# Modulating the first token tile behind its transposes, by columns, in a fused adaLN block

## The chip, the cores and the metric

The kernel runs on one core of a Trainium2 chip. A core has TensorE (PE, the matrix engine, with its weight loads listed apart as PEld), VectorE (DVE), ScalarE (ACT), GpSimd (POOL) and SyncE (SP, which here issues most DMAs). Each engine works through its own instructions in program order, and waits on semaphores where it needs another engine's result. The metric is device time of one execution in microseconds, lower is better; the time of before is the median of three runs.

## The reference

One token matrix x (2048 tokens by 448 channels, float32) goes through two sub-blocks, each with adaptive layer norm. Only the first one's beginning matters here:

```
mod = (silu(c) @ w_mod)                     # c: 1x448, w_mod: 448 x (6*448)
sa, ca, ga, sb, cb, gb = six rows of 448    # sa: shift, ca: scale of the first norm
h = layernorm(x) * (1 + ca) + sa            # modulated tokens
q, k, v = h @ wqkv                          # 16 heads of 28
pq, pk = phi(q), phi(k)                     # phi(t) = t+1 if t > 0 else exp(t)
o = (pq @ (pk^T v)) / (pq . sum(pk))        # linear attention
x = x + ga * (o @ wo)
```

The second sub-block (layer norm, modulation, a token-mixing MLP with 2048 -> 1792 -> 2048) comes after it and isn't touched.

## The kernel before

The tokens are 16 tiles of 128 rows. For each tile t the stage works like this: statistics on DVE with a power on POOL (`a_stats`, L283), two DVE passes that normalise and modulate by rows (`a_norm_a` L296: (x - mean) times the scale vector; `a_norm_b` L302: times 1/std plus the shift vector), a small duplicate on ACT (`a_dup` L307), four transposes on PE (`a_transpose` L312), a split of the transposed tile into a high and a low part in a rounded float format (`a_split` L318: high `hh` on ACT, low `hl` on DVE), and then products with the key weights (`kp`) and query weights (`qp`), eleven matmuls each (`project` L324). The weights are split in the same way: `w_high` (L196, ACT) makes `wh`, `w_low` (L200, DVE) makes `wl`; `w_low_dma` does one of them by ACT and a POOL DMA. Keys go through `a_exp` (ACT) and `a_pk` (DVE), queries through `phi_q` (L353: two ACT activations `eq`, `rq` and a DVE sum `pq`). `a_high` (L382) makes high and low parts of the token-major tile (`xh`, `xl`), `a_pk_parts` those of the keys, and `a_outer` (L415) accumulates their product over the tiles (`cacc`).

Before all that the two vectors have to be made from w_mod: scale (mod 1) and shift (mod 0). Each is a sum of four pieces of 112 rows by 448 columns. `mod_acc` (L159) adds up pieces 0 to 2 on DVE, each weighted by silu(c) per row; `mod_sum` (L173) then adds over the rows with a matmul of ones, which leaves the vector in every one of the 128 rows of a PSUM bank. The fourth piece goes in as a second matmul, with silu(c) spread over 128 columns (`scb`) in place of ones. `mod_out` copies the result to SBUF.

Tile 0 is handled apart, in full float32 (`project0` L448: four matmuls, each of which the trace lists as two instructions). It is modulated by rows as the others, in two column ranges (`a_cols` L436) that read the shift straight from PSUM, then transposed (`a_first`), and copied by ACT (`a_copy` L444) to `h0t`. Until the data is there, `keep_warm` (L140) lets PE multiply ones by ones: 12, then 10, 5 and twice 2 such matmuls, two passes each.

The order of the work is written out by hand from L456 to L592: calls in this order put instructions into the engines' queues. The first lines, L456 to L536, treat tiles 0 to 4 one by one; from L540 a loop over t = 3 .. 15 has the same steps in each turn. SP's loads are issued ahead: x of tile 0, w_mod for the scale, for the shift, x of tile 1, key weights, x of tile 2, query weights, and more tiles.

Of the kernel before, what the change touches and what calls it, by code (L numbers as in the profile page):

```python
# [14 lines left out]
P = 128  # L15
# [9 lines left out]
PRE_LOAD = {12: 2, 13: 4, 14: 6, 15: 8}  # L25
KV_LAG = 3
Q_EARLY = (3, 4)
DVE_LOW = (0, 1, 13, 14, 15)
AHEAD = 8
LAG = 5  # L30
# [2 lines left out]
MOD_AT = {11: [(4, 0)], 12: [(4, 1)], 13: [(4, 2)], 14: [(4, 3)], 15: [(3, 0), (3, 1)]}  # L33
QS = {0: 2, 4: 2}
WARM = 12
WARM2, WARM3 = 10, 5
ACT_STATS = ()
PRE = 9
MID = 5
# [6 lines left out]
def block_kernel(ctx: ExitStack, tc: tile.TileContext, x, wqkv, wo, w1, b1, w2, b2, c, wmod, out):  # L46
# [16 lines left out]
    def slot(name, w=D, dt=F32, parts=P):  # L63
        return slots.tile([parts, w], dt, name=name, tag="slot", padded_shape=[P, 512])
# [8 lines left out]
    def bank(name):  # L73
        return psum.tile([P, 512], F32, name=name, tag="bank")
# [65 lines left out]
    def keep_warm(n):  # L140
        for i in range(n):
            nc.tensor.matmul(warm[:, :P], ones, ones, start=True, stop=True)  # L142
# [12 lines left out]
    def mod_out(j, ps):  # L155
        mods[j] = cst.tile([P, D], F32, name=f"mod{j}")
        nc.scalar.activation(mods[j], ps[:, :D], AF.Copy, bias=1.0 if j in (1, 4) else 0.0)

    def mod_acc(j, n=4):  # L159
        acc = (tslot if j == 5 else slot)(f"acc{j}", parts=G)  # L160
        nc.vector.tensor_scalar_mul(acc, wm[j, 0], sc[:, 0:1])
        for k in range(1, n):
            nc.vector.scalar_tensor_tensor(acc, wm[j, k], sc[:, k:k + 1], acc, op0=ALU.mult, op1=ALU.add)
        macc[j] = acc

    def mod_part(j, k):
        if k == 0:
# [5 lines left out]
    def mod_sum(j, n=4):  # L173
        ps = bank(f"modp{j}")
        todo = [(scb[:, (k - 2) * P:(k - 1) * P], wm[j, k]) for k in range(n, 4)]
        todo.insert(1, (ones[:G, :], macc.pop(j)))
        for k, (a, b) in enumerate(todo):
            nc.tensor.matmul(ps[:, :D], a, b, start=(k == 0), stop=(k == len(todo) - 1))
        return ps
# [98 lines left out]
    def a_moments(t):  # L278
        b6 = small.tile([P, 6], F32, name=f"st{t}", tag="st")
        nc.vector.bn_stats(b6, X[t])  # L280
        return b6

    def a_stats(t, b6=None):  # L283
        if t in ACT_STATS:
            a_rstd(t, a_mean(t))
            return
        b6 = a_moments(t) if b6 is None else b6
        mv = small.tile([P, 2], F32, name=f"mv{t}", tag="mv")
        nc.vector.bn_aggr(mv, b6)
        ve = small.tile([P, 1], F32, name=f"ve{t}", tag="ve")  # L290
        nc.vector.tensor_scalar_add(ve, mv[:, 1:2], EPS)  # L291
        rs = small.tile([P, 1], F32, name=f"rs{t}", tag="rs")
        nc.gpsimd.tensor_tensor(rs, ve, mhalf[:, 0:1], op=ALU.pow)  # L293
        st[t] = (mv[:, 0:1], rs)

    def a_norm_a(t):  # L296
        h = slot(f"h{t}", 512) if t else h0
        nc.vector.scalar_tensor_tensor(h[:, :D], X[t], st[t][0], mods[1],
                                       op0=ALU.add if t in ACT_STATS else ALU.subtract, op1=ALU.mult)
        hs[t] = h  # L300
# [6 lines left out]
    def a_dup(t):  # L307
        nc.scalar.activation(hs[t][:, D:], hs[t][:, 384:D], AF.Copy)
# [41 lines left out]
        nc.vector.scalar_tensor_tensor(dst, e, 1.0, r, op0=ALU.min, op1=ALU.add)  # L350
        return dst

    def phi_q(ps, name):  # L353
        dst, e, r = slot(f"p{name}"), slot(f"e{name}"), slot(f"r{name}")
        nc.scalar.activation(e, ps, AF.Exp)
        nc.scalar.activation(r, ps, AF.Relu)
        nc.vector.scalar_tensor_tensor(dst, e, 1.0, r, op0=ALU.min, op1=ALU.add)
        return dst

    pq = [None] * NT  # L360
    qps = {}

    def a_q(t):
# [2 lines left out]

    def a_phi_q(keep=0):
        for t in sorted(qps)[:len(qps) - keep]:
            pq[t] = phi_q(qps.pop(t), f"q{t}")


    xss, pks = {}, {}
# [2 lines left out]
    def low(t, lo, full, hi):  # L375
        if t in DVE_LOW:
            nc.vector.tensor_sub(lo, full, hi.bitcast(F32))
        else:
            nc.scalar.activation(lo, hi.bitcast(F32), AF.Copy, scale=-1.0)
            nc.gpsimd.dma_start(lo, full, accum_op=ALU.add)  # L380

    def a_high(t):  # L382
        h = hs[t]
        xss[t] = (slot(f"xh{t}", 512, F32R), slot(f"xl{t}", 384, F32R))
        hi, lo = xss[t]
        nc.scalar.activation(hi[:, :D], h[:, :D], AF.Copy)
        nc.vector.tensor_sub(hi[:, D:], h[:, 384:D], hi[:, 384:D].bitcast(F32))
        low(t, lo, h[:, :384], hi[:, :384])

    pkf = {}  # L390

# [37 lines left out]
        nc.vector.tensor_scalar_mul(scb[:, k * P:(k + 1) * P], ones[:G, :], sc[:, k + 2:k + 3])  # L429

    h0t = slot("h0t", 512)
    h0 = slot("h0", 512)
    nc.vector.memset(h0[:, D:], 0.0)
    raw_t = {}

    def a_cols(c0, c1, sa):  # L436
        h = hs[0]
        nc.vector.scalar_tensor_tensor(h[:, c0:c1], h[:, c0:c1], st[0][1], sa[:, c0:c1], op0=ALU.mult, op1=ALU.add)

    def a_first(chs):  # L440
        for ch in chs:
            nc.tensor.transpose(tps[0][:, ch * P:(ch + 1) * P], hs[0][:, ch * P:(ch + 1) * P], ident)

    def a_copy(chs):  # L444
        s = slice(chs[0] * P, (chs[-1] + 1) * P)
        nc.scalar.activation(h0t[:, s], tps[0][:, s], AF.Copy)

    def project0(j, name, between):  # L448
        ps = bank(f"{name}0")
        for ch in range(4):  # L450
            nc.tensor.matmul(ps[:, :D], h0t[:, ch * P:(ch + 1) * P], raw_t[j][ch], start=(ch == 0), stop=(ch == 3))
            if ch == 1:
                between()
        return ps[:, :D]

    raw_t = {j: [raw_w[j, ch] for ch in range(4)] for j in (0, 1)}  # L456
    a_stats(0)
    mod_acc(1, 3)
    keep_warm(WARM2)
    mod_out(1, mod_sum(1, 3))  # L460
    mod_acc(0, 3)
    keep_warm(WARM3)
    a_norm_a(0)
    moments1 = a_moments(1)
    a_stats(1, moments1)
    sap = mod_sum(0, 3)
    keep_warm(2)
    a_cols(0, 256, sap)
    a_cols(256, D, sap)
    tps[0] = bank("tp0")  # L470
    a_first((0, 1))
    a_first((2, 3))
    keep_warm(2)
    w_high(1, 0)
    a_copy((0, 1))
    a_copy((2,))
    a_copy((3,))
    del tps[0]
    st.pop(0)
    a_norm_a(1)  # L480
    w_high(1, 1)
    a_norm_b(1, sap[:, :D])
    a_dup(1)
    w_low(1, 0)
    w_high(1, 2)
    w_low(1, 1)
    kp0 = project0(1, "kp", lambda: a_transpose(1))
    a_stats(2)
    a_split(1)
    w_high(1, 3)  # L490
    w_high(0, 0)
    w_low_dma(0, 0)
# [10 lines left out]
    a_stats(3)  # L503
    a_dup(2)
    a_pk(0, kp0)
    qps[0] = project0(0, "qp", lambda: a_transpose(2))
    a_split(2)
    a_norm_a(3)
    a_exp(1, kp1)
    a_norm_b(3)  # L510
    a_dup(3)
    w_low(0, 2)
    w_low(0, 3)
    kp2 = project(2, 1, "kp")
    a_high(0)
    a_pk(1, kp1)
# [1 line left out]
    qps[1] = project(1, 0, "qp", True)  # L518
    del heads[1]
    a_split(3)  # L520
    a_stats(4)
    a_phi_q(1)
    a_high(1)
    a_norm_a(4)
    a_exp(2, kp2)
    a_norm_b(4)
    a_pk_parts(0)
    a_dup(4)
    a_pk(2, kp2)
    a_phi_q()  # L530
    a_pk_parts(1)
    a_q(2)
    a_high(2)
# [6 lines left out]
    for t in range(3, NT):  # L540
        kp = project(t, 1, "kp")
        if t + 1 < NT:
            a_transpose(t + 1)
        a_outer(t - KV_LAG)
        if t in Q_EARLY:
            a_q(t)
        if t == 10:
            mp = mod_sum2(2)
        if t + 1 < NT:
            a_split(t + 1)  # L550
        if t + 2 < NT:
# [24 lines left out]
        if 5 <= t < 9:  # L576
            mod_part(2, t - 5)
        if t == 9:
            mod_split(2)
        if t in (10, 11):  # L580
            load_mod(14 - t)
        if t == 4:
            for g in range(4):
                w = tslot(f"wo{g}", parts=G)
                nc.sync.dma_start(w, wo[g * G:(g + 1) * G, :])
                wo_sb.append(w)
            load_qkv(2, tslot)
# [568 lines left out]
```

## Time and profile before

| | |
|---|---|
| runs | 443.7, 443.97, 444.35 us, median 443.97 |
| profiled execution | 444.42 us |
| its span (first to last instruction) | 442.7 us |
| granted clock in the span | 1.000 |
| HBM read / written | 41.88 MB / 7.34 MB, 111 GB/s over the span |

The span is the part of the execution between the first and last instruction that the profile holds; 1.7 us lie around it. In a timeline row the first number is the start, the second the time from the start of the first to the end of the last instruction of the row, then engine, line, operation, output and inputs, the count, and in brackets how long the engine sat idle before it and what ended that. In a list of groups "x16 | 12.1, 759" means 16 instructions, 12.1 us in all, 759 ns each. In a list of waits "a <- b: us in total, times, longest us". In the chain of work that ended last each piece has start, time and what it was.

### The profile page before, as it was taken

The numbers are of one execution on the slowest core, as the hardware profiler recorded it, in microseconds if no ns is written. First come the engines' busy times: TensorE is split into PE (matmuls) and PEld (weight loads), VectorE is DVE, ScalarE is ACT, GpSimd is POOL, SyncE is SP. The second block draws the span as 40 slices with busy tenths as digits, with TensorE's granted clock in tenths as the row PEclk, the third lists the DMA queues.
The fourth block names the chain that finished last, engine by engine and source line by source line (L and its number), as shares of the span: only waits on it lengthen the run. The fifth ranks groups of instructions, "written<-read, shape, count | busy, mean of one in ns | idle before, by whom it ended". The sixth has DMA issues, their size and how long they took to land.

```text
span 442.7 us, 7285 instructions
## 1 busy us (share of the span) xinstructions
PE 437.4 (99%) x2405; PEld 404.6 (91%) x2405; DVE 366.7 (83%) x795; ACT 262.1 (59%) x560; POOL 119.7 (27%) x192
## 2 busy tenths in 40 slices
PE   8999999999999999999999999999999999999996
PEld 8689999999899999988999999999999999999996
DVE  5897788887899999997469676539999988898894
ACT  2659878655655676777666255226675555655550
POOL 2114576630014456664300000010112220231110
PEclk9999999999999999999999999999999999999999
DMA  8959899993330003322417555476667977977430
GB/s 224 298 151 185 149 190 222 233 273 127 118 100 2 24 25 105 64 50 49 142 30 246 164 177 161 139 190 182 154 159 189 181 160 182 187 161 204 73 53 33
DMA packets 65046, 63.70 MB, mean 144 GB/s; under 512 B 8880, under 2 KB 57328, under 8 KB 65008
## 3 DMA queue, kind: packets, MB, share of 16 engines
q1 hardware_dynamic: 55072, 47.63, 36.1%
q0 software_dynamic: 9936, 15.60, 22.2%
q8 instruction: 19, 0.31, 0.3%
q14 instruction: 19, 0.16, 0.1%
HBM read 41.88 MB, written 7.34 MB: 111 GB/s over the span
## 4 chain that ended last, share of the span: by engine, by line
PE 88%; DVE 9%; issue 1%; ACT 1%; DVEq 0%
PE y L972 19%; PE y L973 9%; PE up L773 9%; PE up L772 9%; PE up L771 8%; PE cacc L424 8%; PE kp L337 7%; PE qp L337 7%; PE op L721 4%; PE warm L142 2%; PE tp L316 2%; DVE y L744 1%; DVE pn L686 1%; DVE ptl L709 1%; DVE y L740 1%
## 5 line engine op out<-in xcount | busy, mean ns | idle before, releaser
L773 PE MATMUL up<-h2h,pl 128*128 128x448 f32 x224 | 81.3, 363 | 0.0
L772 PE MATMUL up<-h2l,ph 128*128 128x448 f32 x224 | 81.2, 363 | 0.0
L771 PE MATMUL up<-h2h,ph 128*128 128x448 f32 x224 | 80.7, 360 | 0.0
L932 POOL DMA_DIRECT2D a<-a x16 | 14.1, 966 | 144.9 <-DMA a<-in_B_w_dram 75.5
L772 PEld LDWEIGHTS up<-h2l,ph 128*128 128x128 f32 x224 | 42.0, 188 | 3.2
L771 PEld LDWEIGHTS up<-h2h,ph 128*128 128x128 f32 x224 | 41.9, 187 | 3.0
L78 DVE TENSOR_TENSOR pl<-pr,ph 128x512 fp32r<-128x512 f32 x52 | 35.1, 686 | 11.5 <-ACT ph L77 8.6
L773 PEld LDWEIGHTS up<-h2h,pl 128*128 128x128 f32 x224 | 42.0, 188 | 2.2
L77 ACT ACTIVATE ph<-pr 128x512 fp32r<-128x512 f32 x52 | 31.6, 628 | 17.8 <-PE up L772 7.3
L994 ACT ACTIVATE cc<-y 128x448 f32<-128x448 f32 x24 | 12.9, 544 | 23.2 <-PE y L973 23.2
L424 PE MATMUL cacc<-pkh,xh 128*128 128x448 f32 x64 | 24.2, 379 | 0.0
L424 PE MATMUL cacc<-pkl,xh 128*128 128x448 f32 x64 | 23.1, 362 | 0.0
L721 PE MATMUL op<-oh,pth 128*128 128x448 f32 x60 | 23.0, 383 | 0.0
L1015 POOL DMA_DIRECT2D out_dram<-yt x14 | 12.7, 905 | 35.8 <-DVE yt L1001 26.2
L337 PE MATMUL kp<-wh,hh 128*128 128x448 f32 x60 | 22.1, 374 | 0.0
L721 PE MATMUL op<-oh,ptl 128*128 128x448 f32 x60 | 21.7, 362 | 0.0
L337 PE MATMUL qp<-wh,hh 128*128 128x448 f32 x60 | 21.6, 365 | 0.0
L337 PE MATMUL kp<-wh,hl 128*128 128x448 f32 x60 | 21.5, 363 | 0.0
L337 PE MATMUL qp<-wh,hl 128*128 128x448 f32 x60 | 21.4, 362 | 0.0
L293 POOL TENSOR_TENSOR rs<-ve,mhalf 128x1 f32<-128x1 f32 x16 | 15.0, 939 | 21.7 <-DVE ve L291 21.1
L679 POOL TENSOR_SCALAR den<-den 128x16 f32<-128x16 f32 x16 | 8.8, 550 | 41.9 <-DVE den L676 41.9
L889 DVE TENSOR_TENSOR u<-u,mod 128x448 f32<-128x448 f32 x14 | 8.7, 620 | 11.9 <-ACT u L888 11.7
(216 smaller groups left out, 1351.6 us busy)
## 6 DMA issues: line engine op xcount, KB each, us to landing
pr<-in_B_w_dram SPq DMA_DIRECT2D x56, 256.0 KB, 2.9
a<-in_B_w_dram SPq DMA_DIRECT2D x32, 256.0 KB, 4.3
a<-in_B_w_dram SPq DMA_DIRECT2D x32, 192.0 KB, 4.3
wm<-in_w_mod_dram SPq DMA_DIRECT2D x24, 196.0 KB, 4.7
x<-in_A_x_dram SPq DMA_DIRECT2D x16, 224.0 KB, 4.4
out_dram<-x SPq DMA_DIRECT2D x14, 224.0 KB, 2.0
out_dram<-yt POOLq DMA_DIRECT2D x14, 224.0 KB, 4.7
pk<-pk POOLq DMA_DIRECT2D x12, 224.0 KB, 4.8
```

What stands on the lines that cost most here:

```text
L77: nc.scalar.activation(hi, full, AF.Copy)
L78: nc.vector.tensor_sub(lo, full, hi.bitcast(F32))
L293: nc.gpsimd.tensor_tensor(rs, ve, mhalf[:, 0:1], op=ALU.pow)
L337: nc.tensor.matmul(o, a[:, ch * P:(ch + 1) * P], b, start=(n == 0), stop=(n == 10))
L424: nc.tensor.matmul(cacc[ch][:, :D], a[:, s], b, start=(t == 0 and i == 0), stop=(t == NT - 1 and i == len(todo) - 1))
L721: nc.tensor.matmul(opb[t][:, :D], a[:, g * P:(g + 1) * P], b, start=(n == 0), stop=(n == len(todo) - 1))
L771: nc.tensor.matmul(ps[:, :D], hi[:, sl], mh, start=first, stop=False)
L772: nc.tensor.matmul(ps[:, :D], hi[:, sl], ml, start=False, stop=False)
L773: nc.tensor.matmul(ps[:, :D], lo[:, sl], mh, start=False, stop=last)
L932: nc.gpsimd.dma_start(w, a, accum_op=ALU.add)
L972: nc.tensor.matmul(ps[:, :D], h[:, s], w, start=opens and r == r0, stop=False, skip_group_check=True)
L973: nc.tensor.matmul(ps[:, :HD], l[:, s], wh, start=False, stop=closes and r == PAIRS - 1 - (LAST if (q, m) == (NP - 1, 6) else 0), skip_gro ...
```

## The change

Tile 0 no longer goes through the row-wise modulation before its transposes. DVE makes the plain normalised tile `xn0` as soon as its statistics are there; PE transposes that; and since channels are then partitions, scale and shift become one number per partition. `col_sum` makes these numbers: for each of four 128-channel ranges a matmul with the accumulated piece as weights and a single column of ones, into a bank `colp`; ACT copies them to `cols` (two copies for each vector, as the last range only uses its upper 64 partitions). `a_mod` then modulates a transposed chunk in one ACT activation with a scale and a bias per partition, out of PSUM into `h0t`. The row-wise vectors are still made, for the other tiles.

All four pieces now go into the accumulator (`MODN`), so that `mod_sum` is one matmul; the first term is made on ACT (`mod_acc`), the other three on DVE (`mod_rest`). The filler counts go from 10 and 5 to 6 and 2, and the two twos go. ACT converts the first key weights only after tile 0's chunks and the duplicate of tile 1. The row-wise modulated tile 0, which `a_high` needs later, is made on DVE behind the statistics of tile 4, which in turn move ahead of `kp` of tile 2. Tile 4's two passes move ahead of tile 1's low parts, tile 1's high part on ACT moves up, and the duplicate of tile 4 moves behind the queries of tile 1. The DVE sums of the queries of tiles 0 to 2 (`phi_q_sum`) are put off to turns 5 to 7 of the loop.

```diff
+QLATE = 2
+MODN = (4, 4)
+MOD_ACT = (0, 1, 2, 3)
...
-WARM2, WARM3 = 10, 5
+WARM2, WARM3 = 6, 2
...
+    def mod_acc(j):
+        acc = slot(f"acc{j}", parts=G)
+        nc.scalar.activation(acc, wm[j, 0], AF.Copy, scale=sc[:, 0:1])
+        macc[j] = acc
+
+    def mod_rest(j):
+        acc = macc[j]
+        for k in range(1, 4):
             nc.vector.scalar_tensor_tensor(acc, wm[j, k], sc[:, k:k + 1], acc, op0=ALU.mult, op1=ALU.add)
...
+    CH = [(0, P), (P, 2 * P), (2 * P, 3 * P), (D - P, D)]
+    cols = cst.tile([P, 64], F32, name="cols")
+    nc.gpsimd.memset(cols, 0.0)
+    colp = bank("colp")
...
+    def col_sum(j):
+        at = 0 if j else 4
+        todo = [(macc[j], ones[:G, 0:1])] + [(wm[j, k], sc[:, k:k + 1]) for k in range(MODN[j], 4)]
+        for n, (w, v) in enumerate(todo):
+            for c, (c0, c1) in enumerate(CH):
+                nc.tensor.matmul(colp[:, at + c:at + c + 1], w[:, c0:c1], v, start=(j == 1 and n == c == 0),
+                                 stop=True, skip_group_check=True)
+        for p0, c0, c1, mod in ((0, 0, 3, (0, 1)), (64, 3, 4, (2, 3))):
+            nc.scalar.activation(cols[p0:, at + c0:at + c1], colp[p0:, at + c0:at + c1], AF.Copy, bias=float(j))
+            if j == 0:
+                for ch in mod:
+                    a_mod(ch)
...
+    def a_first():
+        tps[0] = bank("tp0")
+        for ch, (c0, c1) in enumerate(CH):
+            nc.tensor.transpose(tps[0][:, ch * P:(ch + 1) * P], xn0[:, c0:c1], ident)
...
+            nc.scalar.activation(h0t[:, s], tps[0][:, s], AF.Identity, scale=scale, bias=bias)
...
     a_stats(0)
-    mod_acc(1, 3)
+    xn0 = slot("xn0")
+    nc.vector.tensor_scalar(xn0, X[0], st[0][0], st[0][1], op0=ALU.subtract, op1=ALU.mult)
+    mod_acc(1)
+    mod_acc(0)
+    mod_rest(1)
+    a_first()
     keep_warm(WARM2)
-    mod_out(1, mod_sum(1, 3))
-    mod_acc(0, 3)
+    col_sum(1)
+    mod_out(1, mod_sum(1, MODN[1]))
+    mod_rest(0)
     keep_warm(WARM3)
-    a_norm_a(0)
-    moments1 = a_moments(1)
-    a_stats(1, moments1)
-    sap = mod_sum(0, 3)
-    keep_warm(2)
-    a_cols(0, 256, sap)
-    a_cols(256, D, sap)
-    tps[0] = bank("tp0")
-    a_first((0, 1))
-    a_first((2, 3))
-    keep_warm(2)
-    w_high(1, 0)
-    a_copy((0, 1))
-    a_copy((2,))
-    a_copy((3,))
-    del tps[0]
-    st.pop(0)
+    a_stats(1)
     a_norm_a(1)
-    w_high(1, 1)
+    col_sum(0)
+    sap = mod_sum(0, MODN[0])
     a_norm_b(1, sap[:, :D])
     a_dup(1)
+    w_high(1, 0)
+    w_high(1, 1)
+    kp0 = project0(1, "kp", {1: lambda: a_transpose(1)})
+    del tps[0]
     w_low(1, 0)
+    a_stats(2)
+    a_split(1)
     w_high(1, 2)
     w_low(1, 1)
-    kp0 = project0(1, "kp", lambda: a_transpose(1))
-    a_stats(2)
-    a_split(1)
...
     a_exp(1, kp1)
+    a_high_act(1)
     a_norm_b(3)
     a_dup(3)
     w_low(0, 2)
     w_low(0, 3)
+    a_stats(4)
+    a_norm_a(0)
+    a_norm_b(0)
     kp2 = project(2, 1, "kp")
...
     a_split(3)
-    a_stats(4)
+    a_norm_a(4)
+    a_norm_b(4)
     a_phi_q(1)
-    a_high(1)
-    a_norm_a(4)
+    a_high_low(1)
     a_exp(2, kp2)
-    a_norm_b(4)
     a_pk_parts(0)
-    a_dup(4)
     a_pk(2, kp2)
     a_phi_q()
+    a_dup(4)
...
+        if 5 <= t <= 5 + QLATE:
+            phi_q_sum(t - 5)
```

More of the change, by code (lines that the diff above doesn't have):

```diff
@@ L157, in mod_out @@
         nc.scalar.activation(mods[j], ps[:, :D], AF.Copy, bias=1.0 if j in (1, 4) else 0.0)
[L159 to L162, printed above, removed]
+    def mod_acc(j):
[5 more added lines that the diff above has]
+        for k in range(1, 4):
             nc.vector.scalar_tensor_tensor(acc, wm[j, k], sc[:, k:k + 1], acc, op0=ALU.mult, op1=ALU.add)
-        macc[j] = acc
     def mod_part(j, k):
@@ L175, in mod_sum @@
         todo = [(scb[:, (k - 2) * P:(k - 1) * P], wm[j, k]) for k in range(n, 4)]
-        todo.insert(1, (ones[:G, :], macc.pop(j)))
+        todo.insert(0, (ones[:G, :], macc.pop(j)))
         for k, (a, b) in enumerate(todo):
@@ L296, in a_norm_a @@
     def a_norm_a(t):
-        h = slot(f"h{t}", 512) if t else h0
+        h = slot(f"h{t}", 512)
         nc.vector.scalar_tensor_tensor(h[:, :D], X[t], st[t][0], mods[1],
@@ L351, in phi_k, with phi_q, phi_q_sum @@
         return dst
-    def phi_q(ps, name):
-        dst, e, r = slot(f"p{name}"), slot(f"e{name}"), slot(f"r{name}")
+    def phi_q(ps, name, t):
+        e, r = slot(f"e{name}"), slot(f"r{name}")
         nc.scalar.activation(e, ps, AF.Exp)
         nc.scalar.activation(r, ps, AF.Relu)
-        nc.vector.scalar_tensor_tensor(dst, e, 1.0, r, op0=ALU.min, op1=ALU.add)
-        return dst
-    pq = [None] * NT
+        eqs[t] = (e, r)
+    def phi_q_sum(t):
+        pq[t], (e, r) = slot(f"pq{t}"), eqs.pop(t)
+        nc.vector.scalar_tensor_tensor(pq[t], e, 1.0, r, op0=ALU.min, op1=ALU.add)
+    pq, eqs = [None] * NT, {}
     qps = {}
@@ L368, in a_phi_q @@
         for t in sorted(qps)[:len(qps) - keep]:
-            pq[t] = phi_q(qps.pop(t), f"q{t}")
+            phi_q(qps.pop(t), f"q{t}", t)
+            if t > QLATE:
+                phi_q_sum(t)
     xss, pks = {}, {}
@@ L380, in low, with a_high_act, a_high_low, a_high @@
             nc.gpsimd.dma_start(lo, full, accum_op=ALU.add)
-    def a_high(t):
-        h = hs[t]
+    def a_high_act(t):
         xss[t] = (slot(f"xh{t}", 512, F32R), slot(f"xl{t}", 384, F32R))
-        hi, lo = xss[t]
-        nc.scalar.activation(hi[:, :D], h[:, :D], AF.Copy)
+        nc.scalar.activation(xss[t][0][:, :D], hs[t][:, :D], AF.Copy)
+    def a_high_low(t):
+        h, (hi, lo) = hs[t], xss[t]
         nc.vector.tensor_sub(hi[:, D:], h[:, 384:D], hi[:, 384:D].bitcast(F32))
         low(t, lo, h[:, :384], hi[:, :384])
+    def a_high(t):
+        a_high_act(t)
+        a_high_low(t)
     pkf = {}
@@ L431, in block_kernel, with a_mod @@
     h0t = slot("h0t", 512)
-    h0 = slot("h0", 512)
-    nc.vector.memset(h0[:, D:], 0.0)
     raw_t = {}
[L436 to L446, printed above, removed]
+    CH = [(0, P), (P, 2 * P), (2 * P, 3 * P), (D - P, D)]
[18 more added lines that the diff above has]
+            nc.tensor.transpose(tps[0][:, ch * P:(ch + 1) * P], xn0[:, c0:c1], ident)
+    def a_mod(ch):
+        s = slice(ch * P, (ch + 1) * P)
+        scale, bias = cols[:, ch:ch + 1], cols[:, 4 + ch:5 + ch]
+        if ch in MOD_ACT:
+            nc.scalar.activation(h0t[:, s], tps[0][:, s], AF.Identity, scale=scale, bias=bias)
+        else:
+            nc.vector.tensor_scalar(h0t[:, s], tps[0][:, s], scale, bias, op0=ALU.mult, op1=ALU.add)
     def project0(j, name, between):
@@ L451, in project0 @@
             nc.tensor.matmul(ps[:, :D], h0t[:, ch * P:(ch + 1) * P], raw_t[j][ch], start=(ch == 0), stop=(ch == 3))
-            if ch == 1:
-                between()
+            between.get(ch, int)()
         return ps[:, :D]
@@ L505, in block_kernel @@
     a_pk(0, kp0)
-    qps[0] = project0(0, "qp", lambda: a_transpose(2))
+    qps[0] = project0(0, "qp", {1: lambda: a_transpose(2)})
     a_split(2)
```

## The prediction

> **What bounds the kernel now.** I read the page's first block, then what TensorE (PE) waits for, then the chain that ended last, in order of time. The first block and the list of all of PE's waits:
>
> ```profile
> PE 437.4 (99%) x2405; PEld 404.6 (91%) x2405; DVE 366.7 (83%) x795; ACT 262.1 (59%) x560; POOL 119.7 (27%) x192
> ```
>
> ```profile
> PE warm L142 <- DVE mhalf L96: 1.1, 1, 1.1
> PE tq L701 <- DVE pn L686: 0.4, 1, 0.4
> PE tp L442 <- DVE h L438: 0.2, 1, 0.2
> ```
>
> PE is busy for 437.4 of 442.7 us and waits for 1.7 us in all. But busy isn't useful: the chain shows that the first 15 us are mostly filler.
>
> ```profile
> 1.11 7.92 PE warm L142 x44
> 9.03 1.51 PE modp L178 x4
> 10.53 1.12 PE warm L142 x10
> 11.65 1.52 PE modp L178 x4
> ...
> 14.56 0.45 PE warm L142 x4
> 15.03 1.77 PE kp L451 x4
> 16.80 0.44 PE tp L316 x4
> 17.24 1.51 PE kp L451 x4
> 18.75 2.21 PE kp L337 x11
> ...
> 31.47 2.20 PE kp L337 x11
> ```
>
> The lines to keep are the "warm" ones, which compute nothing, and 15.03, where the first product on tokens (kp of tile 0) starts. From there PE works without a gap, apart from the 0.4 us at tq, to the end. So the time is "when kp of tile 0 starts" plus a fixed stream of PE work plus any new wait in that stream. The change moves the start; it neither adds to nor takes from the stream behind 15.03. The question is how much sooner the start comes, and whether the engines that feed PE can follow.
>
> **The change part by part.** First, when the start can come. It needs the shift vector (mod 0), hence the sum over four pieces of w_mod on VectorE (DVE).
>
> ```profile
> 6.75 1.40 DVE L163 SCALAR_TENSOR_TENSOR acc<-wm,sc,acc 112x448 f32<-112x448 f32 x2 [1.20 <-DMA wm<-in_w_mod_dram]
> 8.46 0.45 DVE L161 TENSOR_SCALAR acc<-wm,sc 112x448 f32<-112x448 f32 x1 [0.31 <-DMA wm<-in_w_mod_dram]
> 9.23 1.45 DVE L163 SCALAR_TENSOR_TENSOR acc<-wm,sc,acc 112x448 f32<-112x448 f32 x2 [0.32 <-DMA wm<-in_w_mod_dram]
> ```
>
> These sums wait for data: 6.75, 8.46 and 9.23 are arrivals. Now ScalarE (ACT) makes both first terms, and DVE takes three terms in place of two. One costs 0.68 and starts 0.72 to 0.77 behind the one before (1.40 and 1.45 less 0.68). For mod 1: 6.75 + 2 x 0.72 + 0.68 = 8.9; that is before 9.2, so it doesn't delay mod 0, whose three terms run from 9.23 to about 11.4. (The normalised tile xn0, one pass of the kind of the 0.45 row, fits in the idle 1.20 us before 6.75.) The last piece must be in by 10.7:
>
> ```profile
> wm<-in_w_mod_dram SPq DMA_DIRECT2D x2, 196.0 KB, 5.5
> 4.57 0.89 SPq L112 DMA_DIRECT2D wm<-in_w_mod_dram  x2
> x<-in_A_x_dram SPq DMA_DIRECT2D x1, 224.0 KB, 5.3
> 9.92 0.36 SPq L105 DMA_DIRECT2D x<-in_A_x_dram  x1
> ```
>
> The last two pieces are issued by 5.0 and land 5.5 later, 10.5. It is in time. The loads' order on the SP queue isn't touched.
>
> From 11.4 PE makes the column sums: four matmuls with one column, eight passes. No row shows one; I price a pass at 0.11, as the four transposes at 16.80 (0.44) and the ten warm passes at 10.53 (1.12) have it, since there too every pass loads 128 columns of weights. 8 x 0.11 = 0.9, to 12.3. Bounds: 0.06 a pass, half of that because next to nothing streams (0.5 in all), and 0.17 (1.4 in all), the mean weight load (404.6/2405 in the first block) with nothing beside it. Then ACT:
>
> ```profile
> L762 ACT ACTIVATE y<-y,nb,rt 128x448 f32<-128x448 f32 x16 | 12.1, 759 | 10.2 <-POOL nb L761 10.2
> L386 ACT ACTIVATE xh<-h 128x448 fp32r<-128x448 f32 x16 | 9.0, 565 | 0.0
> L446 ACT ACTIVATE h0t<-tp 128x128 f32<-128x128 f32 x2 | 0.4, 278 | 0.0
> L148 ACT ACTIVATE ec<-c_sb 112x4 f32<-112x4 f32 x1 | 0.2, 206 | 0.5 <-DMA c_sb<-in_c_dram 0.5
> ```
>
> ```profile
> 14.88 0.44 ACT L446 ACTIVATE h0t<-tp 128x128 f32<-128x128 f32 x2
> ```
>
> Column copy: 0.21 (the 112x4 row). Modulation of a 128x128 chunk: 0.278 for the chunk, plus 759 - 565 = 194 ns for a scale and a bias read per partition: 0.47. The two chunks of 0.278 take 0.44 together, so the next starts 0.12 before the last one ends; with 0.47 that is a start each 0.35. Some 0.2 us later (my estimate for the last pass to drain and ACT to be told) the copy starts at 12.5, the first chunk is done at 13.25, and **kp of tile 0 starts at 13.3, 1.7 us before 15.03**. The sum for mod 0 on PE (one matmul of 0.76 now) ends at 13.1, beside it. The removed warm passes, memset and second modulation on DVE are gone from the path; the transposes of tile 0 run near 6.5, when PE has only filler.
>
> The Trainium skill, "ScalarE: Activation LUTs", section "What ACT_TABLE_LOAD costs", lets neighbouring activations overlap by about 93 ns. No run here shows two neighbours with two pointer operands; by that figure each chunk would follow after 0.37 and the gain below would be some 0.06 less.
>
> Second, whether DVE follows. The two conversions of key weights that DVE needs (wh, L198; each an activation of the kind of the 0.565 row) stood on ACT ahead of tile 0's copies; they now stand behind four chunks, a second column copy and the duplicate of tile 1. ACT starts: chunks 12.8 and 13.15, copy 13.5, chunks 13.75 and 14.1, duplicate 14.45, wh 14.6, done 15.2. DVE sits idle from about 13.85 (tile 1 done) to 15.2, a new wait. Behind it on DVE, in order: the low part wl, statistics of tile 2 (its data is in at 9.92 + 5.3 = 15.2), then the low half hl of tile 1.
>
> ```profile
> 15.37 1.15 DVE L204 TENSOR_TENSOR wl<-wr,wh 128x448 fp32r<-128x448 f32 x2
> 17.91 0.69 DVE L78 TENSOR_TENSOR hl<-tp,hh 128x512 fp32r<-128x512 f32 x1 [0.45 <-ACT hh L77]
> 21.77 0.62 DVE L280 BATCH_NORM_STATS2 st<-x 128x6 f32<-128x448 f32 x1
> 22.71 0.62 DVE L350 SCALAR_TENSOR_TENSOR pk<-ek,rk 128x448 f32<-128x448 f32 x1
> 23.56 0.69 DVE L78 TENSOR_TENSOR hl<-tp,hh 128x512 fp32r<-128x512 f32 x1 [0.23 <-ACT hh L77]
> 28.00 0.68 DVE L78 TENSOR_TENSOR hl<-tp,hh 128x512 fp32r<-128x512 f32 x1
> 30.67 0.68 DVE L298 SCALAR_TENSOR_TENSOR h<-x,mv,mod 128x448 f32<-128x448 f32 x1
> 31.46 0.69 DVE L304 SCALAR_TENSOR_TENSOR h<-h,rs,mod 128x448 f32<-128x448 f32 x1
> 32.07 0.62 DVE L400 SCALAR_TENSOR_TENSOR pkl<-pk,pkh 128x448 fp32r<-128x448 f32 x1
> ...
> 53.74 0.69 DVE L78 TENSOR_TENSOR hl<-tp,hh 128x512 fp32r<-128x512 f32 x1 [0.34 <-ACT hh L77]
> ```
>
> From the rows: wl takes 0.54, statistics 0.94 (21.77 to 22.71), a tile's two passes 1.40 (30.67 to 32.07). So hl of tile 1 starts at 15.2 + 0.54 + 0.94 = 16.7, against 17.91: DVE gains only 1.2. From there to hl of tile 3 DVE took 28.00 - 17.91 = 10.09, with 0.31 of waiting for ACT in it (23.56 less 22.71 and 0.54). The new order puts more in between: one wl (0.54) that was earlier, statistics of tile 4 (0.94), both passes over tile 0 (1.40 - they now run on DVE with the others, since ACT made only the transposed copy), and a wait: the high part of tile 0 (0.565 on ACT) can't start before those passes end, and DVE waits for it, about 0.6. The waiting of 0.31 goes. So 10.09 + 0.54 + 0.94 + 1.40 + 0.6 - 0.3 = 13.3, and hl of tile 3 runs from 30.0 to 30.75.
>
> PE, meanwhile, comes 1.7 sooner, so to the product kp of tile 3 at 31.47 - 1.7 = 29.8, whose third matmul reads hl 0.4 later. First it waits about 0.3 in kp of tile 1 for the last low weights (DVE: hl and three low parts behind it, at 0.54 to 0.69 each, from 16.7 to about 19.1; PE would be there at 13.3 + 1.77 + 0.44 + 1.51 + 1.8 = 18.8), then about 0.4 at tile 3. **The sum: third matmul of tile 3 at 30.8 in place of 31.87, so 1.1 us sooner**: 1.7 - 0.3 - 0.3. What comes next has room: tile 4's two passes moved ahead of tile 1's parts; their result is due at 31.47 + 2.20 - 1.1 = 32.6 and done at 30.0 + 0.6 + 0.8 + 0.7 = 32.1.
>
> At nothing I cost: three sums pq moved to later turns (0.62 each, on DVE, which waits for ACT there, 0.34 in the row at 53.74, while PE is further back still; without that cover up to 0.6 each); the first terms on ACT, which has no other work ahead of the column copies (without the cover 0.66 each); the memset and the power of tile 4's statistics (L293) on POOL, busy for 27% of the span. The longer life of three pairs of tiles holds slots; loads of later x tiles might wait for one, a few us before they are due; bound 0 to 0.3.
>
> The profiled execution took 444.42 us, 0.45 over the median 443.97. 444.42 - 1.1 = 443.3 there, and against the median **442.9**.
>
> **The rivals.**
> *PE sets it, not DVE* (442.2). If the chunks overlap better on ACT (a start each 0.16, as the rows without pointers have it) wh comes 0.6 sooner and hl of tile 3 is in time: the gain is the 1.7, or 2.1 with column sums at 0.5. For it: no row shows the pointers' spacing. Against: 194 ns a piece have to go somewhere.
>
> *The gain is eaten* (443.4). With 0.17 a pass the column sums end 0.5 later, everything behind them too, and the gain is 0.6. For it: with one column nothing covers a weight load. Against: four transposes in 0.44.
>
> *PE loses its rate* (445.8, the slower side). The trace has two rates for the same pass:
>
> ```profile
> 1.11 0.80 PE L142 MATMUL warm<-ones 128*128 128x128 f32 x2 [1.11 <-DVE mhalf L96]
> 1.11 1.01 PE L142 MATMUL warm<-ones 128*128 128x128 f32 x3 [1.11 <-DVE mhalf L96]
> ```
>
> At the start a pass adds 0.21, from 10.53 on 0.11. With 44 passes in 7.92 the turn lies at about 28 x 0.21 = 5.9 us after the first, at 7.0. Now PE stands idle near 6.3, 8.8 and 11, and streams single columns. If a slow stretch of 5.9 us falls on the work behind 11.4, it costs half, 2.9, less the 1.1: +1.8. It decides from 2.2 us of slow stretch on. Against: each gap is under half a microsecond. The granted clock reads 1.00 throughout, also before 7.0, so that column can't warn of it.
>
> The Trainium skill, "TensorE: Matmul & The Clock Gate", Part 1, has a free-running window of about 3.4 us, busy or idle, that sets full or half clock, and Part 4 says that transposes don't count as busy the same way. By it a dull window around 10 to 13 us would give 3.4 us at half rate, 1.7 us, and a total of about 444.5. The two rates agree with it; nothing in this trace shows a fall back.
>
> That the change doesn't do what it says (a chunk that waits for all four, for one) costs up to 1.0 and ends among the eaten gains.
>
> **How the numbers follow.** Forecast 0.48, PE sets it 0.22, eaten 0.18, lost rate 0.12. About 0.2% (0.9 us) is what a measurement can tell from none. Of the forecast's own spread (gain 0.5 to 1.5) some 65% lies beyond it: faster 0.48 x 0.65 + 0.22 = 0.53, same 0.17 + 0.18 = 0.35, slower 0.12. The range runs from PE's best (2.1: 441.9) to an eaten gain with late slots (444.2), and leaves the lost rate out.
>
> **What would show it.** kp of tile 0 at 13.3 (12.9 to 13.9); eight column passes in 0.9; modulated chunks of 0.47 on ACT; DVE idle about 1.3 before wl; a PE wait for wl near 19 and one for hl near 30.4; then no new one. A kp start after 14.2, passes of 0.21 behind 9 us, or PE waiting in the later turns for VectorE would make it wrong.

## The result, and the profile after

| | before | after |
|---|---|---|
| runs in one comparison | 22 | 22 |
| median, us | 444.35 | 445.28 |
| lowest to highest, us | 443.7 to 444.95 | 443.5 to 448.35 |
| profiled execution, its span, us | 444.42, 442.7 | 444.36, 442.7 |
| granted clock of the profiled execution | 1.000 | 0.996 |

After over before is 1.0024 [1.0014, 1.0035]: a little slower, where 442.9 and faster was forecast, and above the forecast range, which ends at 444.2. The spread says more than the median: after has runs below the fastest of before, and runs 3 us above its slowest. Each run comes with the mean clock granted to TensorE, and sorts by it. Here are the 22 runs with the 12 of a second comparison of the same kernel (e11 below):

| granted clock of the run | runs of 34 | median, us | lowest to highest |
|---|---|---|---|
| 0.998 to 1.000 | 14 | 444.26 | 443.5 to 445.28 |
| 0.995 to 0.996 | 11 | 445.32 | 444.36 to 446.26 |
| 0.991 to 0.992 | 9 | 446.82 | 446.52 to 448.35 |

Of the 97 runs of before whose clock is listed none is under 0.998. A mean of 0.996 over 442 us is what 0.004 x 442 x 2 = 3.5 us at half rate make; 0.992 is twice that. So two things are to be explained: stretches at half rate, with about 1.1 us between the first two groups of runs and 1.5 between the next two, and that even at full rate after is only about 0.1 us ahead of before.

The first block of after answers to that of before: PE is as busy as it was, although 11 of 31 filler matmuls have gone.

```profile
PE 436.8 (99%) x2395; PEld 403.1 (91%) x2395; DVE 367.5 (83%) x794; ACT 264.9 (60%) x567; POOL 120.2 (27%) x193
```

The chain that ended last, of after, from the start of the products on tokens (start, time, what):

```profile
9.53 0.87 PE modp L184 x2
...
12.12 1.60 PE modp L184 x2
13.72 2.46 PE kp L486 x4
16.61 1.50 PE kp L486 x4
18.12 2.30 PE kp L343 x11
...
31.06 2.35 PE kp L343 x11
...
69.63 2.21 PE kp L343 x11
```

The first half of kp of tile 0 starts at 13.72 in place of 15.03, but takes 2.46 where its equal took 1.77 before, and the sum for the shift vector (modp, at 12.12) takes 1.60 where the same two passes for the scale vector, at 9.53, took 0.87. The stretches of after show why. The columns are the time of the stretch, busy time of PE, PEld, DVE, ACT and POOL with instructions, the granted clock, the DMA share and GB/s:

```profile
11.00:12.00 1.00, 0.90 (x9) 0.93 (x9) 0.93 (x4) 0.00 (x0) 0.03 (x1) 1.00 1.07 303
12.00:13.00 1.00, 1.00 (x4) 0.49 (x4) 0.48 (x1) 0.81 (x3) 0.90 (x1) 0.55 1.07 278
13.00:14.00 1.00, 1.00 (x2) 0.49 (x2) 0.19 (x1) 0.95 (x4) 0.00 (x0) 0.50 1.07 335
14.00:15.00 1.00, 1.00 (x2) 0.34 (x1) 0.49 (x1) 0.67 (x3) 0.00 (x0) 0.50 1.07 378
15.00:16.00 1.00, 1.00 (x3) 0.48 (x2) 0.72 (x2) 0.71 (x2) 0.00 (x0) 0.74 1.07 269
16.00:17.00 1.00, 1.00 (x7) 0.80 (x6) 0.78 (x3) 0.35 (x1) 0.07 (x1) 1.00 1.09 276
```

The third number from the right is the clock: 0.50 from 12.1 to about 15.5, then 1.00 for the rest. PE is "busy" all the time, with two instructions a microsecond at 13 and 14 and seven at 16. The trace of before has 1.00 in the same stretches. What PE did ahead of it (timeline of after):

```profile
8.48 1.05 PE L462 MATMUL colp<-ones,acc 112*128 112x1 f32 x8
9.39 1.00 PE L184 MATMUL modp<-acc,ones 112*128 112x448 f32 x2
10.23 0.61 PE L145 MATMUL warm<-ones 128*128 128x128 f32 x4
11.10 1.02 PE L462 MATMUL colp<-ones,acc 112*128 112x1 f32 x8 [0.26 <-ACT mod L160]
11.98 1.74 PE L184 MATMUL modp<-acc,ones 112*128 112x448 f32 x2
```

In the 3.4 us ahead of 12.1, passes of 128 or 448 columns fill some 1.5 us; the rest is passes that stream one column ("112x1"), and a gap of 0.26. The Trainium skill, "TensorE: Matmul & The Clock Gate", Part 1, has a free-running window of about 3.4 us that decides between full and half clock; the length of the stretch agrees with it. The same page of the Trainium skill, section "Why this matters for your kernels", asks for no idle gap of over about 3 us. That isn't enough here: no gap of PE after the first matmul and before 12 is over 0.41 us.

### The profile page after: what moved, and what is told of

It is laid out like the page before. It is cut to its first block, busy times and chain, and to the rows that moved or that the text cites. A ratio compares the mean times of both kernels' runs of the same rounds, so it can differ in the third digit from the quotient of the medians.

```text
span 442.7 us, 7275 instructions
## 1 busy us (share of the span) xinstructions
PE 436.8 (99%) x2395; PEld 403.1 (91%) x2395; DVE 367.5 (83%) x794; ACT 264.9 (60%) x567; POOL 120.2 (27%) x193
## 4 chain that ended last, share of the span: by engine, by line
PE 87%; DVE 9%; issue 1%; ACT 1%; DMA 0%; POOL 0%; DVEq 0%; ACTq 0%
PE y L1005 19%; PE y L1006 9%; PE up L804 9%; PE up L806 9%; PE up L805 8%; PE cacc L440 8%; PE kp L343 8%; PE qp L343 7%; PE op L754 4%; PE tp L322 2%; DVE y L777 1%; DVE pn L719 1%; DVE ptl L742 1%; DVE y L773 1%; DVE x L763 1%
```

## The experiments

Four theories. **A**: PE loses its rate, because passes of one column and gaps look idle (A speaks of the granted clock and of the time that it costs). **B** (rival): the rate is a symptom, the time goes to VectorE's chain and later stages. **C**: the gain of the head is taken back at 45 to 85 us, where transfers bind. **D**: it is lost somewhere else. Each kernel was timed in turn with the kernel before on the same chip; "ratio" is that to before. All figures are medians.

### A against B: the width of the column passes

**e1_wide**: the changed kernel with the column of ones made 128 wide, so that each of the eight passes streams 128 columns; a copy then takes the first of them, and each vector's sums get a bank of their own.

```diff
-        todo = [(macc[j], ones[:G, 0:1])] + ...
+        todo = [(macc[j], ones[:G, :])] + ...
...
-                nc.tensor.matmul(colp[:, at + c:at + c + 1], w[:, c0:c1], v, ...
+                nc.tensor.matmul(colp[:, c * P:(c + 1) * P], w[:, c0:c1], v, ...
```

> The changed kernel, but each of its eight column passes streams 128 columns of ones in place of one (the first column of each range is read). A (PE loses its rate because the column sums and the gaps look idle): the passes take as long as before (about 1.0 us for eight, as the weight load sets them), the granted clock reads 1.000 in nearly every run, the spread falls from 5 us to about 1, kp of tile 0 lasts 3.5 us without its transposes' slow part, and the median falls by at least 1 us against the changed kernel (445.3), to 443.3 or so. B (the rate is a symptom; the time goes to VectorE's longer chain and to later stages): the clock is cured or not, but the median stays within 0.4 us of the changed kernel's runs with clock 1.000, about 444.5.

Measured: 444.64 us (444.04 to 445.46, 11 runs), ratio 1.0006 [0.9997, 1.0014], clock 0.998 to 1.000 in every run. PE idles more than in after, yet keeps its rate:

```profile
9.39 1.16 PE L463 MATMUL colp<-ones,acc 112*128 112x128 f32 x8 [0.61 <-DVE acc L170]
...
12.40 1.16 PE L463 MATMUL colp<-ones,acc 112*128 112x128 f32 x8 [0.65 <-DVE acc L170]
```

So gaps of this size alone don't bring the fall: it takes the narrow passes. The clock is as A says, the time isn't: it is 1.3 us above the 443.3 expected, so something else takes the gain too.

**e2_fill**: the narrow passes stay, more filler around them.

```diff
-WARM2, WARM3 = 6, 2
+WARM2, WARM3 = 10, 5
```

> The changed kernel with the old filler counts (10 and 5 in place of 6 and 2). A: the clock stays at 1.000 more often, but PE is late for the column sums by 0.9 and then 0.4 us, so kp of tile 0 starts near 14.3 and the median is 443.8 to 444.3. B: the filler only delays, 445.3 plus 0.5 to 1.3.

Measured: 444.75 us (443.85 to 445.76), ratio 1.0006 [0.9996, 1.0015], clock 0.998 or more in all 11 runs. Again the rate is held and the time ends between the two expectations. More filler ahead of both column sums is a second cure, with nothing gained on e1.

**e3_before_narrow**: the kernel before, with all filler behind the first 16 matmuls one column wide.

```diff
-    keep_warm(WARM2)
+    keep_warm(4)
+    keep_narrow(WARM2 - 4)
...
-    keep_warm(WARM3)
+    keep_narrow(WARM3)
...
-    keep_warm(2)
+    keep_narrow(2)
```

> The kernel before, in which the filler behind the first 16 matmuls streams one column in place of 128; nothing else differs, and the number of passes is the same. A: the granted clock falls under 0.999 in a good part of the runs, with 3.4 us stretches near 0.5 between 8 and 20 us, and the time rises by 0.5 to 2 us with a wider spread. B: no change, within 0.3 us.

Measured: 444.74 us, ratio 1.0002 [0.9993, 1.0011], clock 0.998 or more in all 11 runs. A miss for A as it was put: narrow filler alone doesn't bring the fall. The timeline of e3 shows what is left of wide work there:

```profile
7.46 1.40 PE L148 MATMUL warm<-ones 128*128 128x1 f32 x12
8.72 1.00 PE L182 MATMUL modp<-wm,scb 112*128 112x448 f32 x2
9.56 0.92 PE L182 MATMUL modp<-acc,ones 112*128 112x448 f32 x2
10.31 1.17 PE L148 MATMUL warm<-ones 128*128 128x1 f32 x10
11.34 1.00 PE L182 MATMUL modp<-wm,scb 112*128 112x448 f32 x2
12.18 0.92 PE L182 MATMUL modp<-acc,ones 112*128 112x448 f32 x2
12.93 0.50 PE L148 MATMUL warm<-ones 128*128 128x1 f32 x4
13.74 0.65 PE L446 MATMUL tp<-ident,h 128*128 128x128 f32 x3 [0.30 <-DVE h L442]
```

From 8.7 to 12.1 that is some 2.4 us of wide passes, against 1.5 in after. But two other stretches of 3.4 us in e3, from 7.5 and from 10.3, hold only some 1.6 us of wide passes each, the second with a gap of 0.30 in it, and e3 keeps its rate. So the share of wide work, counted this way, hardly tells the two kernels apart. What narrow passes need beside them for the fall (their place among the others, their place in time, the last 0.1 us) stays open.

**e9_narrow_early** and **e12_e5_again** came last and give the clean comparison: e12 is the best kernel found below (e5), once more; e9 is the same with the column passes narrow, as the change has them. They differ in nothing but these passes and the bank they write to.

> The changed kernel with w_high(1,0) ahead of col_sum(0) and load_mod(4) in turn 4, and with the column sums as they were changed, one column a pass: it differs from e5_e4_earlymod in the width of the column passes alone. A (TensorE loses its rate because narrow passes and gaps look idle): granted clock 0.992 to 0.996 in at least half of the runs, with a stretch of 0.5 near 12 to 16 us in those, and a median 0.6 to 1.2 us above e12's, 443.9 to 444.5. B (the rate is a symptom): within 0.3 of e12, whatever the clock.

> e5_e4_earlymod unchanged, so that e9 and e10 have it on the same chip. C with A: 443.3 (443.0 to 443.6), clock 0.998 or more in all runs, ratio to the kernel before 0.9963 to 0.9982 again. D: the ratio comes back to 0.999 or more, and the first figure was chance.

Measured: e9 444.69 us (442.33 to 446.87), ratio 1.0004 [0.9987, 1.0021]; e12 443.53 us (442.95 to 445.74), ratio 0.9982 [0.997, 0.9994]; 12 runs each. The clock is 0.992 to 0.996 in 7 of 12 runs of e9 and in none of e12. By clock, e9 has 443.31 us at 0.998 and over (5 runs), 445.15 at 0.995 to 0.996 (5), and 446.55 and 446.87 at 0.992. **The narrow passes cost 1.16 us in the median** (0.6 to 1.2 expected by A; the intervals of the two ratios touch), and runs of e9 that keep the rate are as fast as e12. Every run of e9 under 0.998 is slower than every other. A holds, and B as it was put falls, though at full rate after is only 0.1 us faster than before, which is what C and D are about. The fall hits some runs of the same program and not others, and e9's profiled run keeps its rate with the same passes. Where a stretch of 3.4 us begins could decide that, or when w_mod arrives in a run; no run tells them apart. If late arrivals bring both the fall and a late start, the differences between the groups by clock are more than the price of the slow stretch alone; the comparison of e9 with e12 has this problem less, since both have the same loads.

**e11_after_again**: the changed kernel, unchanged.

> The changed kernel, unchanged. A: granted clock below 0.998 in over half of its runs, median 445.0 to 445.6, single runs to 447 and above; the runs at full clock 0.7 to 1.5 us below the others. B: no connection between clock and time.

Measured: 445.18 us (443.61 to 448.22), ratio 1.0023 [1.0005, 1.0041]; clock under 0.998 in 6 of 12 runs, a little less than expected; medians 444.34, 445.49 and 446.98 by clock, in the order that A wants and further apart than the 0.7 to 1.5 expected. Its profiled run (0.995) fell too, some 0.7 us later than after's, behind a gap of PE of 0.84:

```profile
12.06 1.15 PE L462 MATMUL colp<-ones,acc 112*128 112x1 f32 x8 [0.84 <-DVE acc L170]
```

```profile
12.00:13.00 1.00, 0.94 (x8) 0.97 (x8) 0.93 (x4) 0.00 (x0) 0.07 (x1) 0.91 1.11 249
13.00:14.00 1.00, 1.00 (x3) 0.59 (x4) 0.45 (x1) 0.72 (x3) 0.86 (x1) 0.50 1.08 238
...
16.00:17.00 1.00, 1.00 (x4) 0.38 (x3) 0.53 (x1) 0.91 (x2) 0.00 (x0) 0.89 1.14 253
```

No profiled run had a clock of 0.992, so where the second stretch lies in those wasn't seen.

### C against D: where the rest went

**e4_wide_wh**: e1, with the first conversion of key weights on ACT put ahead of the column sums of the shift vector, since the prediction had DVE wait for it.

```diff
+    w_high(1, 0)
     col_sum(0)
...
-    w_high(1, 0)
```

> e1_wide with the first conversion of the key weights moved on ScalarE ahead of the column copies for the shift, where ScalarE waits. A together with the forecast's account of VectorE (its chain from the first wl to hl of tile 3 sets PE): VectorE's wait of 0.8 before wl goes, hl of tile 3 comes 0.5 to 0.8 sooner than in e1_wide, PE's waits in kp of tiles 1 and 3 shrink, and the median is 0.3 to 0.6 below e1_wide. B, if later stages hand the gain back: e1_wide and this one agree within 0.2, whatever happens before 35 us.

Measured: 444.16 us (443.23 to 445.89), ratio 0.999 [0.9977, 1.0004]; 0.48 below e1, as expected, though the two intervals overlap. In its trace DVE goes on without the wait, and kp of tile 3 starts at 30.73, 0.74 sooner than before. Yet the span is 443.1. Most of the gain went here (waits of PE in e4, then the row itself):

```profile
PE cacc L440 <- DMA pkl<-pk: 0.6, 1, 0.6
```

```profile
82.04 0.45 PE L440 MATMUL cacc<-pkh,xh 128*128 128x448 f32 x1
83.14 0.47 PE L440 MATMUL cacc<-pkl,xh 128*128 128x448 f32 x1 [0.65 <-DMA pkl<-pk]
```

pkl, the low part of the keys, is finished by a DMA of POOL, and PE waits for its landing: 1.10 us from one row to the next, where the matmuls around it follow every 0.20.

**e7_e4_nosum** and **e8_before_nosum**: e4 and before, without the POOL transfers that add pk into the sum of keys. These two leave out the sum of keys of tiles 2 to 13.

```diff
-        else:
-            nc.gpsimd.dma_start(pksum[t % 2], pk, accum_op=ALU.add)
```

> e4_wide_wh without the accumulating transfers of pk into pksum on the POOL queue (the sum of the keys of tiles 2 to 13 is left out). C (the head's gain is handed back because the transfers between 45 and 85 us, above all those on the POOL queue, set the pace there: in e4_wide_wh PE is 0.7 us ahead of the kernel before at 31 us and 0.6 behind at 85, with waits for pkl's transfer): the waits for pkl go, and this kernel stays 0.7 to 1.3 us below e8_before_nosum to the end. D (the gain is lost elsewhere, or never was there): it differs from e8_before_nosum by less than 0.4.

> The kernel before without the same transfers (the sum of the keys of tiles 2 to 13 is left out). C: 0 to 0.5 us under the kernel before, as PE waits for a transfer there seldom. D: the same.

Measured: e7 443.81 us, ratio 0.9981 [0.9971, 0.999]; e8 444.09, ratio 0.9985 [0.9976, 0.9993]. e7 is 0.28 below e8; C expected 0.7 to 1.3 and D under 0.4, so here C misses and D is met. Fewer transfers help both kernels, before even a little more (by 0.0015 of its time, over the 0.5 us that both theories allowed; e4 by 0.0009). So these are not the transfers that take the new head's gain.

**e5_e4_earlymod** and **e6_before_earlymod**: e4 and before, with nothing left out, but the load of the four pieces of w_mod for a later vector issued in turn 4 of the loop in place of turn 10.

```diff
-        if t in (10, 11):
-            load_mod(14 - t)
+        if t == 11:
+            load_mod(3)
...
         if t == 4:
...
+            load_mod(4)
```

> e4_wide_wh with the four loads of w_mod for vector 4 issued in turn 4 in place of turn 10, so that they travel at 34 to 42 us, when the transfer engines are idle, and not at 65 to 70. All of the work is done. C: pkl's transfer of tile 9 lands sooner, PE's waits near 83 us shrink from 1.5 to under 0.5, and the median is 0.5 to 1.2 below e4_wide_wh (444.2), about 443.3. D: no change, 444.2.

> The kernel before with the same loads moved. C: within 0.3 us of the kernel before, since PE isn't ahead there. D: the same.

Measured: **e5 443.30 us (442.64 to 444.15), ratio 0.9973 [0.9963, 0.9982]**; e6 444.20, ratio 0.9995 [0.9987, 1.0003]. The move is worth nothing measurable to before. To the new head it is worth 0.9 us by the medians of e4 and e5, which come from different comparisons; by the ratios it is 0.75, and with e12, which is e5 again, 0.4, and the intervals overlap. So the size is loose; the direction is C's, with another transfer than e7 took away, and the traces show the mechanism. From 34 to 42 us, where the expectation calls the transfer engines idle, they move 82 GB/s in e4 and 197 in e5; from 65 to 70 it is 228 and 181. The same transfer of pkl in four traces (its POOL issue, then the time from issue to landing, all between 74 and 80 us), first before:

```profile
L403 POOL DMA_DIRECT2D pkl<-pk x1: 857/857/857, 76.4 to 76.4; - x1
...
DMA to landing us min/median/max: 5.8/5.8/5.8
```

```profile
82.65 0.36 PE L424 MATMUL cacc<-pkl,xh 128*128 128x448 f32 x1
```

It lands at 76.4 + 5.8 = 82.2 and is read at 82.65: **before has 0.4 us of room there, and no more**. A head that is 1.1 us sooner can't keep that at turn 10 unless the transfer comes sooner as well. It doesn't. After issues it at 76.3 and e4 at 76.5 (the row of before has 76.4), although PE is 0.2 ahead at tile 10 in after, and it lands later:

```profile
L419 POOL DMA_DIRECT2D pkl<-pk x1: 854/854/854, 76.3 to 76.3; - x1
...
DMA to landing us min/median/max: 6.3/6.3/6.3
```

```profile
82.63 0.47 PE L440 MATMUL cacc<-pkl,xh 128*128 128x448 f32 x1
```

76.3 + 6.3 = 82.6: read as it lands, with the weight load waiting 0.3 for it. e11, which is late (0.5 at tile 3) and waits all the same:

```profile
L419 POOL DMA_DIRECT2D pkl<-pk x1: 857/857/857, 77.2 to 77.2; - x1
...
DMA to landing us min/median/max: 6.9/6.9/6.9
```

```profile
84.15 0.48 PE L440 MATMUL cacc<-pkl,xh 128*128 128x448 f32 x1 [0.58 <-DMA pkl<-pk]
```

77.2 + 6.9 = 84.1. And e12, with the four pieces out of the way:

```profile
L419 POOL DMA_DIRECT2D pkl<-pk x1: 854/854/854, 74.9 to 74.9; - x1
...
DMA to landing us min/median/max: 5.2/5.2/5.2
```

```profile
82.05 0.36 PE L440 MATMUL cacc<-pkl,xh 128*128 128x448 f32 x1
```

Issued 1.5 sooner than before and landed at 80.1, 1.9 ahead of its use. As e11 loses although it is late, it isn't the lead alone: in the new order the transfer also lands later after its issue (6.3 in after, 6.9, 6.6 in e4). Which step of the new order does that wasn't taken apart, and with one profile of each kernel chance isn't ruled out.

**e10_both_early**: e5 with the next four pieces in turn 4 as well (`load_mod(3)`).

> e5_e4_earlymod with load_mod(3) in turn 4 as well. C (transfers between 45 and 85 us take the head's gain back): 0 to 0.4 below e12, 442.9 to 443.3, with no wait of TensorE on pkl left. D (what e5 gained is all there is): within 0.2 of e12 or above it, since the two pieces now compete with the key transfers of earlier tiles.

Measured: 443.17 us (443.01 to 444.67, 9 runs), ratio 0.9978 [0.9968, 0.9987]; 0.36 below e12 in the same comparison, at the upper end of what C expected; the intervals overlap, so e10 isn't shown to be better than e5. In the profiles of e10 and e12 TensorE doesn't wait for pkl.

How far each profiled run is ahead of before, at five starts in the chain that ended last (kp of tiles 0, 3, 10 and 13 at 15.03, 31.47, 69.84 and 84.82, and the last qp, at 149.07, in us; a blank where the chain leaves the row out):

| | tile 0 | tile 3 | tile 10 | tile 13 | last qp |
|---|---|---|---|---|---|
| after (clock 0.996) | 1.31 | 0.41 | 0.21 | -0.09 | 0.10 |
| e11, the same (0.995) | 0.12 | -0.52 | -0.75 | -1.60 | -1.40 |
| e1 (1.0) | | 0.07 | -0.28 | -0.30 | -0.09 |
| e4 (1.0) | 0.93 | 0.74 | | -0.60 | -0.38 |
| e9 (0.999) | 1.18 | 1.10 | 0.86 | 0.86 | 1.07 |
| e12 (0.999) | 1.01 | 0.79 | 0.60 | 0.60 | 0.81 |
| e10 (1.0) | 1.52 | 1.33 | 1.12 | 1.10 | 1.32 |

Between the first two columns lies what DVE's chain takes and, in after and e11, the slow stretch; the step from tile 10 to 13 is pkl. In the profile of after that is 0.9 and 0.3. e1, with neither a slow stretch nor a wait for pkl, has lost its head by tile 3 all the same: w_mod came late, kp of tile 0 started at 14.31, and DVE waited 1.19 before its first wl, a wait put down to the arrival of the key weights. The differences between e9, e12 and e10 at tile 0 follow the second column sums, which start at 11.97, 12.11 and 11.59 and hang on the arrival of w_mod, of which more below.

## Why the prediction was wrong, step by step

**The step that failed** is the sentence under "What bounds the kernel now": the change "moves the start; it neither adds to nor takes from the stream behind 15.03". It took from it twice. In the profile of after PE runs at half rate from 12.1 to about 15.5, 1.8 us of that behind its own kp start at 13.72. And the stream meets a transfer, pkl near 82.6, that had 0.4 us of room before and has none after, since it is issued no sooner and lands 0.4 us later.

**The rate.** The rival "PE loses its rate" had the mechanism and the side, and 0.12. Its point against ("each gap is under half a microsecond") wasn't the point: e1 has longer gaps and keeps its rate. Narrow passes were named in it, but not weighed as the change's main new load of PE: 16 passes in place of wide filler. Its price from rows was for 5.9 us at the slow rate, 445.8; the stretch is 3.4 us, and one costs 1.1 in the median. The estimate from the window that the Trainium skill, "TensorE: Matmul & The Clock Gate", Part 1, has gave 3.4 us and 444.5, nearer in length. The median is above that, since runs at full rate already stand at 444.26, and some runs have more than one stretch. That "nothing in this trace shows a fall back" was true of the trace of before, and was no evidence, since before has no narrow passes. The clock column, which the prediction gave up on, did show the fall: 0.50 in the rows of after.

**The start** was near. Forecast 0.9 for eight column passes, measured 1.02 to 1.05; a chunk on ACT each 0.35, measured 0.81 for two of 0.45, that is each 0.36; column copy 0.21, measured 0.17; the 0.2 between the last column pass and the copy, which no row of before showed, measured 0.04 (12.12 to 12.16). The Trainium skill, "ScalarE: Activation LUTs", section "What ACT_TABLE_LOAD costs", has an overlap of 93 ns, which made the spacing 0.37 as an estimate; the trace agrees. ACT in after:

```profile
12.16 0.17 ACT L465 ACTIVATE cols<-colp 128x3 f32<-128x3 f32 x1 [1.19 <-PE colp L462]
12.36 0.81 ACT L479 ACTIVATE h0t<-tp,cols 128x128 f32<-128x128 f32 x2
...
14.69 1.02 ACT L204 ACTIVATE wh<-wr 128x448 fp32r<-128x448 f32 x2
16.65 0.60 ACT L80 ACTIVATE hh<-tp 128x512 fp32r<-128x512 f32 x1 [0.94 <-PE tp L322]
```

The first chunk is there at 12.8, so by its data kp could start 0.5 ahead of the forecast 13.3. It starts at 13.72 because modp, at half rate, lies in front of it: 0.7 of its 1.60 is the rate. Luck helped: the sum for the shift vector started at 8.68 in this profile, where 9.23 was taken.

**DVE's chain** was worked out rightly, and the table of forecasts can be laid on its rows of after:

```profile
15.28 0.62 DVE L210 TENSOR_TENSOR wl<-wr,wh 128x448 fp32r<-128x448 f32 x1 [0.79 <-ACT wh L204]
...
17.28 0.69 DVE L81 TENSOR_TENSOR hl<-tp,hh 128x512 fp32r<-128x512 f32 x1 [0.43 <-ACT hh L80]
...
29.43 0.23 DVE L399 TENSOR_TENSOR xh<-h,xh 128x64 fp32r<-128x64 f32 x1 [0.64 <-ACT xh L395]
...
30.58 0.68 DVE L81 TENSOR_TENSOR hl<-tp,hh 128x512 fp32r<-128x512 f32 x1
```

wl at 15.28 (15.2 forecast), the wait for the high part of tile 0 0.64 (0.6), and from hl of tile 1 to hl of tile 3 30.58 - 17.28 = 13.30 (13.3). DVE's wait before wl is 0.79 in place of 1.3, as tile 1's second pass reads the slow modp and ends later. And hl of tile 1 is at 17.28 in place of 16.7: its high part waits 0.94 for the transposes, which stand on PE behind kp of tile 0 at half rate, and DVE waits 0.43 for the high part. So 0.43 us of the slow stretch goes down DVE's chain to tile 3, one way in which a few slow passes on PE become a late tile.

**"Then no new one"**, of PE's waits, was wrong: the wait for pkl near 83. The prediction priced the later turns by PE's and DVE's rows alone and asked of transfers only whether slots come free. The rows for it were in the trace of before.

**The arrivals** were taken as fixed, from one profile. The shift vector's sum starts at 9.23 there. In kernels whose loads have the same order it starts elsewhere (DVE of e5, then of e1):

```profile
9.28 2.13 DVE L170 SCALAR_TENSOR_TENSOR acc<-wm,sc,acc 112x448 f32<-112x448 f32 x3 [0.53 <-ACT acc L164]
```

```profile
10.07 2.27 DVE L170 SCALAR_TENSOR_TENSOR acc<-wm,sc,acc 112x448 f32<-112x448 f32 x3 [0.73 <-DMA wm<-in_w_mod_dram]
```

and kp of tile 0 follows: 13.38 in e5, 14.31 in e1. Before starts kp at 15.01 to 15.05 in its own profile and in those of e6 and e8, as its filler and row-wise passes are in front of it whatever the arrival. The new head hangs on the arrival, so 1.7 at tile 0 was near its best case.

**The size.** e5, with both losses gone and the wait of DVE shortened, shows what the new head can bring: its medians stand at 0.9973 and 0.9982 of before, 0.8 to 1.2 us, where 1.1 was forecast. That isn't the forecast coming true: it takes wide column passes, an earlier conversion and a moved load, none of which the change has, and the conversion shortens a wait that the forecast had counted in.

## What to carry to other kernels

A start that comes sooner is worth what the tightest thing behind it lets through: follow the lead down the later stages, and for each transfer there compare landing with use (issue plus time to landing, against the row that reads it) before giving it to the total. Filler that keeps TensorE at its rate has a function even though it computes nothing. What takes its place should stream as many columns, as long as it isn't known how many are needed (narrow filler cost e3 nothing, narrow sums cost e9 1.16 us); widening a column to 128 costs 0.11 us for eight passes here (1.16 against 1.05). Where single runs of one program spread far more than the other's, sort them by granted clock before reading any median.

## What the runs showed of the hardware that was not expected

- TensorE fell to half clock for about 3.4 us with no gap of PE over 0.41 us ahead of it in the profiled run of after, behind a stretch of that length with some 1.5 us of wide passes in it. In e11 the gap was 0.84. It happened in 20 of 34 runs of the same kernel, once or twice a run as far as the mean clock tells (0.996 or 0.992), and in none of the 23 runs of e1 and e12, whose passes are 128 wide. e7, wide too, keeps its rate behind a gap of 0.81.
- In the trace PE reads as busy during the fall; the granted clock by stretches of 1 us, and the time of equal rows (modp 0.87 and 1.60), are what shows it.
- A pass that streams one column takes 0.13 us (eight in 1.02 to 1.05), hardly less than one of 128 (eight in 1.16).
- A POOL transfer of pkl, 224 KB, took from 3.9 us (e10) to 6.9 us (e11) from issue to landing, in the same stretch of 74 to 80 us.
